# A written instruction order replaced by another: late DMAs and dearer tiling turns in the plan, 96 DMA semaphores

## The chip, the core and the metric

The kernel runs on one core of one Trainium2 chip. The core has five engines with a queue of their own: TensorE (PE in the profile; its weight loads are shown as PEld), VectorE (DVE), ScalarE (ACT), GpSimd (POOL) and SyncE (SP), which issues nearly all DMAs here. The metric is the device time of one execution in microseconds.

## The reference

Four sublayers run one after the other over 2048 tokens of width 448, in bf16: attention, GLU, attention, GLU, with the same weights for both attentions and for both GLUs.

```python
def _A_ref(x, mem0, Wq, Wk, Wv, Wo, seg_len):      # 64 segments of 32 tokens, 16 heads of 256
    mem = mem0                                     # 8 memory rows
    for s in range(n_seg):
        xs = x[:, s * seg_len:(s + 1) * seg_len, :].copy()
        h = jnp.concatenate([mem, xs], axis=1)     # 40 rows
        q, k, v = ...                              # h times Wq, Wk, Wv
        scores = jnp.einsum('bhqe,bhke->bhqk', q, k) * scale
        scores = jnp.where(mask[None, None], scores, -1000000000.0)
        p = _softmax(scores, axis=-1)
        o = jnp.einsum('bhqk,bhke->bhqe', p, v)
        o = jnp.einsum('bhte,hed->btd', o, Wo)
        mem = o[:, :M, :].copy()
        outs.append(o[:, M:, :])
...
def _B_ref(x, W_gate, W_up, W_down):
    gate = ...; up = ...
    h = relu(gate) * up
    return jnp.einsum('bsf,fd->bsd', h, W_down)

x = x + _A_ref(_layernorm(x, axis=-1), ...)
x = x + _B_ref(_layernorm(x, axis=-1), ...)
x = x + _A_ref(_layernorm(x, axis=-1), ...)
x = x + _B_ref(_layernorm(x, axis=-1), ...)
```

The memory rows of a segment need those of the segment before, so the memory's part is a chain of 63 links in each attention layer. The other 32 rows of a segment hang on the chain but not on each other.

## The kernel before

**What is computed where.** The weights are folded first: `weights` loads Wq and Wk, turns them on TensorE (`transposes`, profile lines L1084 and L1085) and multiplies them per head into `A` (`product`, L1102), and Wv with Wo into `Bsb`. After that each head needs `h A h^T` for its scores and `p h B` for its output.

`chain(step)` runs one link of the memory chain for both attention layers together, the second layer `LAG` = 7 segments behind the first. In series: `mT` times `A` into PSUM (L1270), four evictions into `Usb`, small transposes by a selection matrix (`middle`, L1427) with evictions, scores (L1450), a softmax on VectorE and ScalarE, a transpose of the probabilities, the product with the rows (L1514 and L1518), and the product with `Bsb` (L1307), whose four column groups are added to `Osum` and written to `Ohi`. From there the new memory goes back to `mT`, and by small DMAs into the row tiles `HR`. Most steps also carry rows of the second layer that ride along (`Tr`, `Pr`, `PTr`); `PTr` is made by a transposing DMA.

`tiles(step, t)` does the work of a tile of 128 tokens every fourth step: four `att_group` calls (L1603 into `Ug`, scores L1632, softmax in `Tx` and `Px`, a transposing DMA `Tx<-Px`, products L1514 and L1518, output L1670), then `norm` into a `G` tile (two transposing DMAs `G<-xn`) and the GLU (`glu_units` L1692, `glu_down` L1710).

**The tiling of TensorE.** Its matmuls use five shapes of tile (rows x columns): 64x128 for L1603 and L1692, 64x32 for L1270, 128x32 for L1307, 128x64 for some products of weights, and the full 128x128 for the rest. A matmul of another shape than the one before it is called a turn here.

**What sets the order.** `_Sched.add` records every operation with the engines that could run it and what it needs. `schedule` then follows four tables that stand in the source, written by a search outside the kernel:

- `ORDER`: 9235 entries, one per operation. An entry v means operation v // 5 on engine v % 5 (0 TensorE, 1 ScalarE, 2 VectorE, 3 GpSimd, 4 SyncE). It fixes the order on each engine, and which engine evicts a PSUM bank.
- `BANKS`: the PSUM bank of each allocation, in the same order (8 banks).
- `FILLS`: at such a place in the order, so many matmuls on a zeroed tile (`warm`, L178) whose result nobody reads.
- `TURN`: at which step the parts of a tile were recorded.

`emit` puts each engine's operations in that order and adds semaphore waits. All engines run in order: one that waits holds what stands behind it. Each DMA in order of recording gets a semaphore slot, n modulo `N_DMA`, and needs the DMA n - `N_DMA` landed before it is issued:

```python
            if n >= self.N_DMA:
                o.deps[self.dmas[n - self.N_DMA]] = True
```

`turn_dma` (L1044) issues the transposing DMAs `G<-xn`, `Tx<-Px` and `PTr<-Pr` on SyncE, `dma` (L1049) the plain ones.

Of the kernel before, what the change touches and what calls it, by code (L numbers as in the profile page):

```python
# [50 lines left out]
class _Sched:  # L51
# [5 lines left out]
    N_DMA = 48  # L57
# [13 lines left out]
    def add(self, engs, cost, fn, r=(), w=(), prio=None, dma=0, alloc=(), room=(), mode=0, now=None, part=(0, 0), after=()):  # L71
# [46 lines left out]
        if dma:  # L118
            n = len(self.dmas)
            o.slot = n  # L120
            if n >= self.N_DMA:
                o.deps[self.dmas[n - self.N_DMA]] = True
# [157 lines left out]
def bass_interleave_layers__memory_aug_recurrent_mem_tr__glu_gated_reglu__prompt_kernel(  # L280
# [477 lines left out]
FILLS = {1969: (12, 2, 0), 9083: (15, 0, 0), 9211: (7, 0, 0), 9217: (10, 0, 0)}  # L758
# [1079 lines left out]
```

## Time and profile before

| | before |
|---|---|
| median of 3 runs | 1563.47 us (1560.84 to 1564.4) |
| time of the profiled execution | 1558.09 us |
| its span, first to last instruction | 1556.3 us |
| granted TensorE clock in it | 0.998 |
| TensorE busy (matmul) | 1508.1 us |
| VectorE, ScalarE, GpSimd busy | 1127.3, 820.6, 58.0 us |
| moved by DMA | 49.84 MB |

A matmul's end is modelled in the trace, and matmuls overlap: a 64x128 one is shown with 216 ns, but the next starts about 28 ns later. So TensorE's busy time contains short waits, and its cost is read from starts. A wait for several semaphores is put down to what came last by the profile. Where the engine named had long been done, it was another, often a DMA.

### The profile page before, as it was taken

How to read it: one execution, taken by the hardware profiler on the slowest of the kernel's cores; microseconds unless marked ns; L12 is line 12 of the kernel's file. 1: busy time of each engine (PE TensorE's matmuls, PEld its weight loads, DVE VectorE, ACT ScalarE, POOL GpSimd, SP SyncE). 2: the span in 40 equal slices, each digit the busy share in tenths (PEclk: the TensorE clock that was granted, in tenths of full speed). 3: DMA queues.
4: the chain of work that ended last, by engine and by line, in shares of the span. 5: the costliest groups of instructions: out<-in, count | busy, mean ns of one | idle time of the engine just before them, and what ended most of it. 6: DMA issues, size and time to landing. Idle time of an engine off the chain costs nothing.

```text
span 1556.3 us, 84947 instructions
## 1 busy us (share of the span) xinstructions
PE 1508.1 (97%) x38530; PEld 1097.1 (70%) x38530; DVE 1127.3 (72%) x3284; ACT 820.6 (53%) x2297; POOL 58.0 (4%) x241
## 2 busy tenths in 40 slices
PE   8999999999999999999999999999999999999998
PEld 6676766667667677767767676777768676777766
DVE  8755678677876777778776778677776777767764
ACT  6754556455555545445555555555555556544442
POOL 1000000000000000000000000000000000000000
PEclk9999999999999999999999999999999999999999
DMA  9422000100100100101001101001001111010101
GB/s 266 145 81 56 12 22 16 18 17 17 23 16 19 27 18 20 19 21 24 19 20 21 29 13 28 17 20 25 20 18 19 26 17 28 19 18 21 20 18 27
DMA packets 114167, 49.84 MB, mean 32 GB/s; under 512 B 82824, under 2 KB 113808, under 8 KB 113808
## 3 DMA queue, kind: packets, MB, share of 16 engines
q1 hardware_dynamic: 113168, 44.15, 12.5%
q8 instruction: 304, 4.98, 1.3%
q14 instruction: 55, 0.45, 0.1%
q10 hardware_dynamic: 640, 0.26, 0.1%
HBM read 21.35 MB, written 1.84 MB: 15 GB/s over the span
## 4 chain that ended last, share of the span: by engine, by line
PE 85%; DVE 7%; DMA 5%; ACT 1%; issue 1%; SPq 1%; ACTq 0%; DVEq 0%; POOL 0%
PE psG L1670 14%; PE psG L1603 14%; PE psG L1692 11%; PE psC L1307 11%; PE psC L1270 7%; PE psG L1710 5%; PE psG L1270 3%; PE psG L1514 3%; PE psG L1102 2%; PE psG L1632 2%; PE psC L1427 2%; DMA Tx<-Px 2%; PE psC L1450 1%; PE psC L1514 1%; PE psG L1427 1%
## 5 line engine op out<-in xcount | busy, mean ns | idle before, releaser
L1670 PE MATMUL psG<-Bsb,YT 128*128 128x448 bf16 x1288 | 277.3, 353 | 0.0
L273 ACT ACTIVATE Ug<-psG 64x128 bf16<-64x128 f32 (+2 forms) x441 | 156.7, 370 | 88.9 <-PE psG L1603 72.2
L1692 PE MATMUL psG<-G,glu 64*128 64x128 bf16 x5838 | 184.6, 216 | 11.5 <-DMA G<-xn 5.0
L1307 PE MATMUL psC<-Bsb,YTm 128*32 128x448 bf16 (+2 forms) x4144 | 187.6, 333 | 0.9 <-issue 0.5
L1692 PEld LDWEIGHTS psG<-G,glu 64*128 64x128 bf16 x5838 | 172.6, 94 | 22.0 <-issue 7.9
L1603 PE MATMUL psG<-HT,A 64*128 64x128 bf16 x3332 | 175.7, 217 | 0.3 <-ACT Bsb L273 0.3
L1670 PEld LDWEIGHTS psG<-Bsb,YT 128*128 128x128 bf16 x1288 | 111.1, 97 | 91.2 <-issue 9.5
L1270 PE MATMUL psG<-A,mT 64*32 64x448 bf16 x4424 | 173.7, 350 | 0.3 <-issue 0.3
L1270 PE MATMUL psC<-A,mT 64*32 64x448 bf16 x3416 | 152.8, 350 | 1.9 <-DVE Tr L1476 1.0
L1603 PE MATMUL psG<-HX,A 64*128 64x128 bf16 x2499 | 150.1, 217 | 0.0
L1307 PEld LDWEIGHTS psC<-Bsb,YTm 128*32 128x32 bf16 x4144 | 102.5, 97 | 65.2 <-DVE YTm L276 2.3
L276 DVE CAST Ug<-psG 64x128 bf16<-64x128 f32 (+2 forms) x265 | 111.1, 429 | 23.1 <-PE psG L1603 18.9
L1697 ACT ACTIVATE hG<-psG 128x512 bf16<-128x512 f32 (+1 forms) x125 | 67.9, 543 | 105.3 <-PE psG L1692 99.1
L1603 PEld LDWEIGHTS psG<-HT,A 64*128 64x128 bf16 x3332 | 116.9, 95 | 8.9 <-issue 5.3
L1324 DVE TENSOR_TENSOR Osum<-psC,Osum 32x448 f32<-32x448 f32 (+2 forms) x120 | 73.2, 610 | 68.7 <-ACT Osum L1322 65.9
L276 DVE CAST YT<-psG 128x448 bf16<-128x448 f32 x148 | 90.2, 618 | 41.3 <-PE psG L1518 40.2
L273 ACT ACTIVATE YT<-psG 128x448 bf16<-128x448 f32 x214 | 107.7, 540 | 20.5 <-PE psG L1518 18.2
L1270 PEld LDWEIGHTS psC<-A,mT 64*32 64x32 bf16 x3416 | 76.5, 92 | 53.8 <-ACT mT L273 3.0
L1270 PEld LDWEIGHTS psG<-A,mT 64*32 64x32 bf16 x4424 | 90.3, 92 | 22.0 <-ACT mT L273 1.9
L1710 PE MATMUL psG<-glu,hG 128*128 128x448 bf16 x434 | 97.5, 353 | 0.2 <-DVE hG L1698 0.2
L1698 DVE TENSOR_TENSOR hG<-hG,psG 128x512 bf16<-128x512 bf16 (+1 forms) x113 | 68.9, 617 | 39.3 <-ACT hG L1697 38.4
L1603 PE MATMUL psG<-l,A 64*128 64x128 bf16 x2919 | 97.2, 216 | 0.0
(294 smaller groups left out, 2910.8 us busy)
## 6 DMA issues: line engine op xcount, KB each, us to landing
Bsb<-in_A_Wq_dram SPq DMA_DIRECT2D x6, 384.0 KB
Bsb<-in_A_Wk_dram SPq DMA_DIRECT2D x6, 384.0 KB
glu<-in_A_Wv_dram SPq DMA_DIRECT2D x6, 384.0 KB
Tsb<-Ohi SPq DMA_DIRECT2D x128, 7.0 KB
X<-in_A_x_dram SPq DMA_DIRECT2D x16, 112.0 KB
glu<-in_A_Wo_dram SPq DMA_DIRECT2D x4, 448.0 KB
out_dram<-X SPq DMA_DIRECT2D x16, 112.0 KB
glu<-in_B_W_gate_dram SPq DMA_DIRECT2D x14, 112.0 KB
```

Of the source, the lines that this page charges most:

```text
L273: return E.activation(out, i, ACT.Copy, scale=1.0 if scale is None else scale)
L276: return E.tensor_copy(out, i)
L1270: i = E.matmul(ub[v].ap()[32 * j:32 * j + 32, 0:D], lhsT=self.mT[rw, b, :], rhs=self.A[rw, b, a0:a0 + D], start=(b == 0), stop=(b == 6), t ...
L1307: x = E.matmul(bo.ap()[32 * j:32 * j + 32, 0:d1 - d0], lhsT=self.YTm[:, q, :], rhs=self.Bsb[:, chunks[q], d0:d1], start=(i == 0), stop=(i ...
L1324: s.add("dve", dv_cost(n), lambda E, e, j=j, a_=a_, part=part: E.tensor_tensor(a_, part(j), a_, ALU.add), r=[bo], w=w, part=(j, 0), **P)
L1514: return E.matmul(ps[:, n * q:n * q + n], lhsT=HR[rows, KM + 128 * q:KM + 128 * q + 128], rhs=PT, start=True, stop=True, tile_position=(b, 0))
L1603: i = E.matmul(ub[v].ap()[:, 128 * n:128 * n + 128], lhsT=self.A[rw, b, a0:a0 + 128], rhs=HT[rw, b, :, 0:SEG] if b < 4 else HX[rw, b - 4, ...
L1670: i = E.matmul(bo.ap()[:, 0:D], lhsT=YT[:, c, :], rhs=self.Bsb[:, 14 * g + c, :], start=(g == 0 and c == 0), stop=(g == 3 and c == 13))
L1692: i_ = E.matmul(two[v].ap()[:, 128 * c:128 * c + 128], lhsT=self.Wgu[rw, b, f0:f0 + 128], rhs=G[rw, b, :], start=(b == 0), stop=(b == 6), ...
L1697: s.add("act", 169 + 0.84 * N, lambda E, e, dst=dst, z=two[0], N=N: E.activation(dst, z.ap()[:, 0:N], ACT.Relu), r=[two[0]], w=[("hG", i, ...
L1698: s.add("dve", dv_cost(N), lambda E, e, z=two[1], N=N, dst=dst: E.tensor_tensor(dst, dst, z.ap()[:, 0:N], ALU.mult), r=[two[1]], w=[("hG", ...
L1710: i_ = E.matmul(bk.ap()[:, 0:D], lhsT=hG[:, c, :], rhs=self.Wd[:, c, :], start=(c == 0), stop=(c == NFC - 1))
```

## The change

No operation is added, taken away or resized. Three of the tables and one number are replaced:

- `N_DMA`, the number of DMA semaphores, goes from 48 to 96.
- `ORDER` is written anew by the search, which planned each small DMA to land later than before and counted more for a turn of the tiling. It holds the same 9235 operations. An operation stands 23 places from where it stood before on average (half of them 13 or fewer). 553 operations move from VectorE to ScalarE and 509 the other way, 28 from VectorE to GpSimd and 21 the other way.
- `BANKS` follows the new order (2667 allocations).
- `FILLS` has 2 places instead of 4, 19 matmuls instead of 44.

In the built programs, TensorE's stream has 588 turns after and 574 before. Its first five groups of transposes are those of operations 55, 58, 61, 64 and 81 before, and of 64, 61, 58, 81 and 55 after. (In `ORDER`, 275 is operation 55 on TensorE, 320 is 64.)

```diff
@@ _Sched
-    N_DMA = 48
+    N_DMA = 96
@@ ORDER
-    158, 37, 163, 92, 266, 259, 42, 102, 168, 47, 112, 271, 639, 173, 52, 178, 122, 275, 62, 183, 264, 95, 67, 188,
-    282, 290, 193, 539, 2448, 105, 287, 297, 2453, 544, 305, 302, 72, 312, 549, 320, 317, 327, 554, 405, 332, 559, 77, 345,
...
+    158, 37, 163, 92, 266, 259, 42, 102, 168, 47, 112, 271, 639, 173, 52, 178, 122, 62, 183, 264, 67, 188, 77, 193,
+    72, 539, 82, 2448, 87, 2453, 544, 549, 320, 554, 305, 326, 290, 559, 312, 331, 297, 564, 405, 316, 275, 302, 411, 569,
...
@@ BANKS
-    2, 0, 3, 4, 2, 3, 4, 2, 5, 6, 3, 2, 4, 5, 3, 2, 4, 5, 3, 2, 4, 5, 3, 0, 2, 4, 3, 5, 2, 6, 4, 3, 7, 5, 6, 2, 4, 3, 5, 2,
...
+    2, 3, 4, 5, 2, 3, 0, 4, 1, 2, 5, 3, 4, 6, 2, 3, 4, 5, 2, 3, 4, 5, 2, 3, 4, 2, 3, 5, 6, 7, 3, 4, 2, 5, 6, 0, 2, 4, 3, 5,
...
@@
-FILLS = {1969: (12, 2, 0), 9083: (15, 0, 0), 9211: (7, 0, 0), 9217: (10, 0, 0)}
+FILLS = {1389: (7, 1, 0), 1965: (12, 2, 0)}
```

896 rows, old and new, of tables (BANKS, ORDER) are left out of this document.

## The prediction

> **What bounds the kernel now.** I read the page first: how full each engine is, then its chain.
>
> ```profile
> span 1556.3 us, 84947 instructions
> ...
> PE 1508.1 (97%) x38530; PEld 1097.1 (70%) x38530; DVE 1127.3 (72%) x3284; ACT 820.6 (53%) x2297; POOL 58.0 (4%) x241
> ...
> PE 85%; DVE 7%; DMA 5%; ACT 1%; issue 1%; SPq 1%; ACTq 0%; DVEq 0%; POOL 0%
> ```
>
> TensorE (PE) bounds it everywhere. The change keeps every operation, so what it can move is the time in which PE streams nothing: 1556.3 - 1508.1 = 48.2 us of idle, plus costs that hide inside "busy". The next view groups PE's instructions by line and shape; behind the last bar stands PE's idle time just before the group, and what ended it.
>
> ```profile
> L1692 PE MATMUL psG<-G,glu 64*128 64x128 bf16 x5838 | 184.6, 216 | 11.5 <-DMA G<-xn 5.0 <-ACT Osum L1322 2.4 <-DVE str L1480 1.8
> L1514 PE MATMUL psG<-Tx,HR 40*128 40x128 bf16 x726 | 39.3, 218 | 10.7 <-DMA Tx<-Px 7.5 <-DVE Usb L276 1.3 <-ACT Osum L1322 0.8
> L1514 PE MATMUL psG<-Tx,l 40*128 40x128 bf16 x360 | 19.7, 216 | 3.3 <-DMA Tx<-Px 1.8 <-DVE Ug L276 1.4
> L1514 PE MATMUL psG<-PTr,l 40*128 40x128 bf16 x189 | 14.6, 219 | 1.3 <-DMA PTr<-Pr 1.3
> L1514 PE MATMUL psC<-PTr,l 40*128 40x128 bf16 x183 | 14.2, 217 | 2.5 <-DMA PTr<-Pr 1.7 <-DVE stm L1466 0.3 <-issue 0.2
> L1427 PE MATMUL psG<-Selm,Usb 128*128 128x64 bf16 x424 | 24.4, 193 | 1.0 <-DVE Usb L276 0.8
> ```
>
> The first five groups read a tile that a transposing DMA made: G (the normed tile, for the GLU), Tx (softmax of a tile) and PTr (softmax of a riding step). Before them PE idles 11.5 + 14.0 + 3.8 = 29.3 us, six tenths of all its idle time. Some of it is put down to DVE or ACT. The timeline of one such wait shows why I count that too:
>
> ```profile
> 285.84 2.56 SPq L1044 DMA_TRANSPOSE G<-xn  x2
> ...
> 290.61 0.23 DVE L1480 TENSOR_REDUCE str<-Tr 128x2 f32<-128x80 f32 x1 [0.34 <-ACT Tr L1479]
> ...
> 290.95 1.24 PE L1692 MATMUL psG<-G,glu 64*128 64x128 bf16 x38 [1.79 <-DVE str L1480]
> ```
>
> `glu_units` reads G, the weights and two PSUM banks, never `str`. The reduction merely ended at that moment; what came late was G's second transpose, 290.95 - 285.84 = 5.1 us after the first was issued. So 5.1 us from the pair's issue to its use is the price that an order must cover with other matmuls.
>
> **The change part by part.** *Room for the transposes.* In both written orders I took, for each transposed tile, the matmuls that stand between the last one that feeds it and the first one that reads it, at the intervals of the rows below (L1692 196 in 5.58 us, or 0.028 us each; L1710 ten in 1.90, or 0.190 each), and subtracted the VectorE work that stands between the first and last VectorE operation of that tile's softmax or norm, at the durations of the trace. What is left is the room for queue and landing; the wait above has 4.2 us of it.
>
> G: 12 of 32 readers have under 6 us before, and 9 of those wait; after, 4 of 32 do, and none has under 5 (six before). Tx: 8 of 96 have under 3.5 us before, 2 after; but between 3.5 and 5 there are 16 before and 23 after. PTr: 7 of 62 under 3.5 before, 3 after. With the mean wait of each class of room in the trace before, put on the counts after, G goes from 11.5 to 3.2 us, Tx from 14.0 to 11.6, PTr from 3.8 to 2.3: **12.2 us less**. Bounds: nothing, if the landings were as late as the new plan fears, and 29.3 if all of it goes.
>
> *What is late next.* Where such a wait goes, PE arrives sooner at whatever follows, and the evictions and softmax chains of the same stretch do not get faster. Of the 48.2 us idle, 5.1 belong to the start (4.75 and 0.39, rows below) and 29.3 to the transposes; the other 13.8 are for VectorE, ScalarE and GpSimd, a third of what is not the start. I let a third of the gain come back in such waits: **+4.1 us**, between 0 and all 12.2.
>
> *Evictions near their readers.* In the written order, 23 of the 396 instruction groups on L1427 (the transposes of the step's `Usb`) stand closer to `Usb`'s evictions than these take, against 14 before. The row above has 1.0 us of idle there; by the count it would be 1.6. The longest of those waits is 0.5 us:
>
> ```profile
> PE psG L1427 <- DVE Usb L276: 0.8, 2, 0.5
> ...
> SPq L1049 <- DMA out_dram<-X: 12.3, 7, 2.6
> ```
>
> 23 times 0.5 would be 11.5, so between +0.6 and +10.5; I take **+2.0**, near the row.
>
> *Turns of the tiling and dummies.* PE's stream changes its tile shape 574 times before and 588 times after: the search did not lower the count. The end of the timeline has the price:
>
> ```profile
> 1532.26 5.47 PE L1670 MATMUL psG<-Bsb,YT 128*128 128x448 bf16 x28
> 1537.66 3.30 PE L1692 MATMUL psG<-G,glu 64*128 64x128 bf16 x112
> ...
> 1542.38 2.07 PE L1710 MATMUL psG<-glu,hG 128*128 128x448 bf16 x10 [0.16 <-DVE hG L1698]
> 1544.28 0.72 PE L178 MATMUL psC<-warm 128*128 128x128 bf16 x10
> 1544.93 5.64 PE L1692 MATMUL psG<-G,glu 64*128 64x128 bf16 x196
> 1550.51 2.82 PE L1710 MATMUL psG<-glu,hG 128*128 128x448 bf16 x14
> ```
>
> 28 matmuls at 0.190 are 5.32 us, but the next shape starts after 5.40: a turn takes about 0.09. Ten dummies (0.056 each) and a turn, 0.65, say the same. 14 more turns: **+1.3 us**. The Trainium skill (TensorEngine Tiling (Array Packing), Key Properties) says that changing the tiling mode drains TensorE, and its page TensorE: Matmul & The Clock Gate (Single matmul latency) has about 166 ns of fixed latency on a matmul that stands alone; if a turn laid all of that bare, 14 would cost, as an estimate from that page, 2.3 us. The rows show about half of it per turn, and the sum uses the rows.
>
> The dummies of `FILLS` go from 44 matmuls to 19. The two fills shown stand where PE waits for the last G; in the order after, 8.3 us of real matmuls stand there, and PE needs 1544.93 - 1537.66 = 7.27 us of cover: **-1.4 us** (25 at 0.056), 0 if the wait stays without them.
>
> *The start.* The first transposes on PE are of other weights than before.
>
> ```profile
> 0.74 1.00 SPq L1049 DMA_DIRECT2D Bsb<-in_A_Wq_dram  x2
> ...
> 1.78 1.02 SPq L1049 DMA_DIRECT2D Bsb<-in_A_Wk_dram  x2
> 1.98 1.27 ACTq L1069 DMA_DIRECT2D Bsb<-in_A_Wk_dram  x2
> ...
> 4.75 0.80 PE L1084 MATMUL psG<-ident,Bsb 128*128 128x128 bf16 x6 [4.75 <-DMA Bsb<-in_A_Wq_dram]
> ...
> 8.36 0.80 PE L1084 MATMUL psG<-ident,Bsb 128*128 128x128 bf16 x6 [0.39 <-DMA Bsb<-in_A_Wq_dram]
> ...
> 9.19 1.37 PE L1102 MATMUL psG<-glu 128*64 128x448 bf16 x12
> ```
>
> Before, PE begins with the first load of Wq, 4.0 us after its issue. After, it begins with the second load of Wk (issued about 2.3) and its tails (about 2.6), so at 6.3 to 6.6, 1.6 to 1.9 later. From 4.75 to 9.19 PE does five groups of seven, 3.75 us of work at the first rows' 0.107 each, so about 0.7 of that stretch is waiting that a later beginning does not repeat: **+1.0 us**, between 0 and 1.9.
>
> *The rest.* 96 DMA semaphores let DMA n be issued before DMA n-48 has landed. SyncE's own waits name one DMA landing, the store of X (12.3 us in 7, row above), and that is the reuse of X's buffer, which stays; PE waits for nothing behind it. I cost it at nothing, with no more than the 2.6 us of its longest wait on either side. 553 evictions move from VectorE to ScalarE and 509 back, 28 to GpSimd and 21 back: VectorE loses 51 of 3284. PE covers that, and it helps the chains that trigger the transposes; no extra credit.
>
> Sum: -12.2 + 4.1 + 2.0 + 1.3 - 1.4 + 1.0 = **-5.2 us**. The profiled execution took 1558.1 us with its span of 1556.3, and would come to 1552.9. It stands 5.4 below the runs' median of 1563.5, so I put the difference on the median: **1558.3 us**.
>
> **The rivals.** *Given back in full.* Each wait that goes is replaced by one as long: -12.2 + 12.2 + 2.9 for the other terms, 1566.4. For it: VectorE is 72% full, and Tx has 25 of 96 readers under 5 us (24 before). Against: G has rooms of 6 us and more for 28 readers, 20 before. It is also the case in which the late plan does not reach the chip.
>
> *Slower: the recurrent step.* 70 steps each run `Usb` through two evictions, L1427, scores and softmax in series. If the new order lets other evictions stand ahead of `Usb`'s, each step grows; at 0.25 us (half the longest wait in the row) that is 17.5 us, -12.2 + 0.9 (start, turns and dummies) + 17.5 = +6.2, **1569.7**. It decides over no change from (12.2 - 0.9) / 70 = 0.16 us per step. Against: only 23 of 396 groups are that near, where it needs every step.
>
> *All the transposes' waits go*, 29.3 us, with a third back: -19.5 + 2.9, **1546.9**. Against: the Tx counts.
>
> **How the numbers follow.** The forecast has 0.48 (own range 1551 to 1563), given back 0.18, slower 0.22, all gone 0.12. 0.2% is 3.1 us, about the 3.6 us by which the three runs before differ. Of the forecast, 0.06 lies within that, so faster 0.54, same 0.24, slower 0.22. The range 1546 to 1571 reaches from the best rival to just past the slower one, and takes in the Usb bound only in part.
>
> **What the profile after would show.** PE's idle before L1692 at 3 to 5 us instead of 11.5, before the Tx groups 10 to 13, before PTr 2 to 3; the first matmul at 6.3 to 6.6; PE busy as before within 3 us, and total idle down by about as much as the span. L1427's idle near 2 to 3 us: if it is over 10, the slower rival holds. If G's idle stays near 11, the rooms were no measure of the waits, and the sum is wrong at its first term.

## The result, and the profile after

| | before | after |
|---|---|---|
| median | 1563.41 us (1560.84 to 1564.4, 4 runs) | 1541.03 us (1539.56 to 1542.56, 4 runs) |
| time of the profiled execution | 1558.09 us | 1540.21 us |
| its span | 1556.3 us | 1538.4 us |
| PE busy | 1508.1 us | 1508.3 us |
| PE idle (span less busy) | 48.2 us | 30.1 us |

The changed kernel takes 0.9859 of the time, with a 95% interval of 0.9842 to 0.9877: 22.4 us less, where 5.2 were forecast. The direction was right; the size was not, and 1541.0 lies below the range.

PE streams for the same time in these two profiles, so in them all of the gain is idle time that went. The page of the changed kernel shows it in the two lines that answer those of before, busy engines and the shares of the chain that ended last:

```profile
span 1538.4 us, 84907 instructions
...
PE 1508.3 (98%) x38505; PEld 1095.8 (71%) x38505; DVE 1117.7 (73%) x3233; ACT 826.9 (54%) x2341; POOL 59.7 (4%) x248
...
PE 91%; DVE 5%; DMA 1%; ACT 1%; SPq 1%; issue 1%; POOL 0%; POOLq 0%
```

In the chain, DMA falls from 5% to 1%. Where it went is seen in PE's groups by line and shape (behind the last bar: the idle before the group, and what ended it):

```profile
L1692 PE MATMUL psG<-G,glu 64*128 64x128 bf16 x5978 | 190.0, 216 | 1.7 <-DVE Ug L276 0.8 <-DMA G<-xn 0.7 <-ACT Tx L1642 0.2
L1514 PE MATMUL psG<-Tx,HR 40*128 40x128 bf16 x714 | 39.9, 218 | 3.2 <-DMA Tx<-Px 2.1 <-DVE Usb L276 0.8
L1427 PE MATMUL psC<-Selm,Usb 128*128 128x64 bf16 x544 | 31.3, 193 | 1.1 <-DVE Usb L276 0.9 <-ACT lnst L1537 0.2
L1427 PE MATMUL psG<-Selm,Usb 128*128 128x64 bf16 x436 | 24.2, 193 | 1.0 <-DVE Usb L276 1.0
L1514 PE MATMUL psG<-Tx,l 40*128 40x128 bf16 x345 | 19.8, 216 | 0.0
L1427 PE MATMUL psG<-Selr,Usb 128*128 128x64 bf16 x304 | 17.6, 193 | 0.5 <-DVE Usb L276 0.5
L1514 PE MATMUL psG<-PTr,l 40*128 40x128 bf16 x192 | 12.9, 219 | 0.6 <-DMA PTr<-Pr 0.4
L1514 PE MATMUL psC<-PTr,l 40*128 40x128 bf16 x180 | 12.2, 216 | 0.0
L1514 PE MATMUL psC<-Tx,HR 40*128 40x128 bf16 x54 | 6.0, 217 | 0.4 <-issue 0.2 <-ACT YT L273 0.2
L1514 PE MATMUL psC<-Tx,l 40*128 40x128 bf16 x39 | 3.5, 217 | 0.8 <-DMA Tx<-Px 0.7 <-ACT YTm L273 0.2
```

A reader is a group of matmuls that reads a transposed tile; where 190 are counted below, it is the first one of each tile. Idle before the readers goes from 29.3 to 6.7 us: G from 11.5 to 1.7, Tx from 14.0 to 4.4, PTr from 3.8 to 0.6. That is 22.6 less, and little comes back: the start has 6.9 us where it had 5.1, and all groups but the readers and the start together have 12.4 where they had 10.9; L1427, which waits for `Usb`, has 2.6 of these, 1.0 before. The rest of PE's idle time lies behind its last matmul: 4.4 us, 3.0 before. The timeline of PE has the start:

```profile
6.86 0.80 PE L1084 MATMUL psG<-ident,Bsb 128*128 128x128 bf16 x6 [6.86 <-DVE Sel L1006]
7.45 0.31 PE L1085 MATMUL psG<-ident,Bsb 128*128 128x128 bf16 x1
```

How one wait went is seen in the two timelines. Before, a Tx tile was ready when L1645 ended (593.37 + 0.32 = 593.69), but SyncE was still at the plain DMAs that stand ahead of its transpose in the written order. The transpose was issued at 595.68, and PE stood idle for 1.77 us until it could read the tile at 598.98, 3.30 us after the issue:

```profile
590.07 1.99 SPq L1049 DMA_DIRECT2D l<-Ohi  x2
592.11 1.80 SPq L1049 DMA_DIRECT2D HR<-xn  x3
...
593.37 0.32 DVE L1645 TENSOR_TENSOR Px<-Tx,stx 128x160 bf16<-128x160 f32 x1
...
593.95 1.67 SPq L1049 DMA_DIRECT2D Tsb<-Ohi  x2
595.68 3.13 SPq L1044 DMA_TRANSPOSE Tx<-Px  x2
...
598.98 0.34 PE L1514 MATMUL psG<-Tx,l 40*128 40x128 bf16 x6 [1.77 <-DMA Tx<-Px]
```

The wait cost more than its 1.77 us. In the 3.41 us after it the granted TensorE clock (PEclk, behind the busy times) was half of what it was before:

```profile
core 0: us, PE busy (x) PEld busy (x) DVE busy (x) ACT busy (x) POOL busy (x), PEclk, DMA share, GB/s
596.38:599.79 3.41, 1.64 (x42) 1.30 (x42) 1.43 (x5) 0.65 (x2) 0.00 (x0) 1.00 0.21 42
599.79:603.20 3.41, 3.41 (x74) 3.41 (x70) 1.48 (x3) 1.21 (x3) 0.00 (x0) 0.51 0.33 72
```

In the changed kernel the transpose of the same tile is issued as soon as the tile is ready, and PE comes to it 23.14 us later:

```profile
557.38 0.30 DVE L1645 TENSOR_TENSOR Px<-Tx,stx 128x160 bf16<-128x160 f32 x1
...
557.71 1.17 SPq L1044 DMA_TRANSPOSE Tx<-Px  x1
...
580.85 0.34 PE L1514 MATMUL psG<-Tx,l 40*128 40x128 bf16 x6
```

### The profile page after: what moved, and what is told of

The parts are those of the page before. It is cut to its first block, busy times and chain, and to the rows that moved or that the text cites. A ratio compares the mean times of both kernels' runs of the same rounds, so it can differ in the third digit from the quotient of the medians.

```text
span 1538.4 us, 84907 instructions
## 1 busy us (share of the span) xinstructions
PE 1508.3 (98%) x38505; PEld 1095.8 (71%) x38505; DVE 1117.7 (73%) x3233; ACT 826.9 (54%) x2341; POOL 59.7 (4%) x248
## 4 chain that ended last, share of the span: by engine, by line
PE 91%; DVE 5%; DMA 1%; ACT 1%; SPq 1%; issue 1%; POOL 0%; POOLq 0%
PE psG L1670 15%; PE psG L1603 15%; PE psG L1692 11%; PE psC L1307 11%; PE psC L1270 8%; PE psG L1710 6%; PE psG L1270 4%; PE psG L1514 3%; PE psG L1102 3%; PE psG L1632 2%; PE psC L1427 2%; PE psG L1307 1%; PE psG L1427 1%; PE psC L1450 1%; PE psG L1084 1%; PE psC L1514 1%
## 5 line engine op out<-in xcount | busy, mean ns | idle before, releaser
L273 ACT ACTIVATE Ug<-psG 64x128 bf16<-64x128 f32 (+2 forms) x428 | 152.4, 372 | 80.2 <-PE psG L1603 64.7
L1692 PE MATMUL psG<-G,glu 64*128 64x128 bf16 x5978 | 190.0, 216 | 1.7 <-DVE Ug L276 0.8
L1692 PEld LDWEIGHTS psG<-G,glu 64*128 64x128 bf16 x5978 | 176.4, 94 | 14.1 <-issue 9.8
L1307 PE MATMUL psC<-Bsb,YTm 128*32 128x448 bf16 (+2 forms) x3864 | 178.0, 336 | 0.7 <-issue 0.5
L1603 PE MATMUL psG<-HT,A 64*128 64x128 bf16 x3244 | 168.6, 216 | 0.6 <-issue 0.5
L1270 PE MATMUL psG<-A,mT 64*32 64x448 bf16 x4284 | 164.7, 350 | 0.6
L1603 PE MATMUL psG<-HX,A 64*128 64x128 bf16 x2433 | 144.0, 216 | 0.1
L1307 PEld LDWEIGHTS psC<-Bsb,YTm 128*32 128x32 bf16 x3864 | 96.0, 97 | 64.4 <-DVE YTm L276 2.9
L276 DVE CAST Ug<-psG 64x128 bf16<-64x128 f32 (+2 forms) x267 | 110.4, 422 | 18.3 <-PE psG L1603 13.8
L1603 PEld LDWEIGHTS psG<-HT,A 64*128 64x128 bf16 x3244 | 112.1, 94 | 8.0 <-issue 5.5
L276 DVE CAST YT<-psG 128x448 bf16<-128x448 f32 x140 | 85.1, 618 | 39.6 <-PE psG L1518 38.6
L1270 PEld LDWEIGHTS psG<-A,mT 64*32 64x32 bf16 x4284 | 85.3, 92 | 22.9 <-ACT mT L273 1.9
```

The source lines that it names most:

```text
L273: return E.activation(out, i, ACT.Copy, scale=1.0 if scale is None else scale)
L276: return E.tensor_copy(out, i)
L1270: i = E.matmul(ub[v].ap()[32 * j:32 * j + 32, 0:D], lhsT=self.mT[rw, b, :], rhs=self.A[rw, b, a0:a0 + D], start=(b == 0), stop=(b == 6), t ...
L1307: x = E.matmul(bo.ap()[32 * j:32 * j + 32, 0:d1 - d0], lhsT=self.YTm[:, q, :], rhs=self.Bsb[:, chunks[q], d0:d1], start=(i == 0), stop=(i ...
L1603: i = E.matmul(ub[v].ap()[:, 128 * n:128 * n + 128], lhsT=self.A[rw, b, a0:a0 + 128], rhs=HT[rw, b, :, 0:SEG] if b < 4 else HX[rw, b - 4, ...
L1692: i_ = E.matmul(two[v].ap()[:, 128 * c:128 * c + 128], lhsT=self.Wgu[rw, b, f0:f0 + 128], rhs=G[rw, b, :], start=(b == 0), stop=(b == 6), ...
```

## The experiments

Comparisons are with runs of the kernel before on the same chip, whose median lay between 1556 and 1564 us. The theories at the beginning: ROOM (more PE work between a tile's last feeding matmul and its reader), QUEUE (transposes stand shorter behind plain DMAs on SyncE), EVICTIONS (the engines that evict were better shared out).

**The semaphores alone.** The old tables with the new number of semaphores.

```diff
-    N_DMA = 48
+    N_DMA = 96
```

> The order before, with 96 DMA semaphores instead of 48 and nothing else. Three theories for the 22 us that the new order saves. ROOM: more matmul time, less VectorE work, between the operations that feed a transposing DMA and the first matmul that reads it. QUEUE: transposes stood behind other DMAs in SyncE's queue (in the trace before, the mean time from ready to issue is 1.27 us for Tx; after, 0.73), part of it through waits for the DMA 48 earlier. EVICTIONS: 51 operations fewer on VectorE. ROOM and EVICTIONS: 1563.4, within 2 us. QUEUE, if the semaphores do it: 5 us or more faster than before.

1556.14 us, ratio 1.0 (0.9976 to 1.0023). The semaphores carry nothing of the gain. They do have a price: PE's idle time behind the last matmul is 4.4 us here instead of 3.0. It is 4.4 to 4.8 in every profile with 96 of them, the changed kernel's too, and 2.9 to 3.4 in every one with 48 (`emit` ends with a wait for each DMA among the last `N_DMA` operations of SyncE). This is also a second profile of the old order: idle before G, Tx and PTr of 7.5, 12.6 and 6.1 us (26.2 in all, against 29.3), so single classes of waits vary from run to run more than their sum.

**Transposes ahead in SyncE's queue.** Each transposing DMA of the old order is moved right behind the last operation that it needs; 38 of 222 pass 85 plain DMAs. The cut shows the edit in outline.

```diff
 ORDER (old tables, N_DMA = 96)
-    ..., plain DMAs, transposing DMA, ...
+    ..., transposing DMA, plain DMAs, ...
```

> The order before with 96 semaphores, and each transposing DMA moved forward in the written order to the place right behind the last operation that it needs; 38 of 222 so pass 85 plain DMAs on SyncE. All other engines keep their order. ROOM: within 3 us of 1563.4. QUEUE: 8 to 15 us faster, 1548 to 1555, with the idle time before L1692 and L1514 down by as much.

1567.58 us, ratio 1.0092 (1.0061 to 1.0123): slower, which neither theory had. The queue did get shorter for Tx (from ready to issue 0.74 us on average, 1.27 before and 0.73 in the changed kernel), yet Tx's idle only fell to 11.9 us:

```profile
L1514 PE MATMUL psG<-Tx,HR 40*128 40x128 bf16 x726 | 39.7, 220 | 9.7 <-DMA Tx<-Px 4.6 <-DVE YT L276 1.9 <-DVE Usb L276 1.3
L1514 PE MATMUL psG<-Tx,l 40*128 40x128 bf16 x360 | 19.9, 218 | 2.2 <-DVE Ug L276 1.5 <-issue 0.7
```

The groups beyond the transposes' readers and the start have 18.9 us of idle instead of 10.9, and PE's busy time is 1516.2 us instead of 1508.1: six stretches at half the clock lie in this profile, two in that of before. That the plain DMAs which were passed are now late is likely, but was not shown wait by wait. QUEUE by itself is not it.

**The engines of the evictions.** The old order, every operation on the engine that the new order gives it (in outline).

```diff
 ORDER (old places, N_DMA = 48)
-    v = 5 * operation + old engine
+    v = 5 * operation + new engine
```

> The order before, but each operation that can run on two engines runs on the engine that the new order gives it (553 from VectorE to ScalarE, 509 the other way, 28 to GpSimd and 21 back), at its old place. ROOM: no gain; 1563 to 1573, since the places were written for other engines. EVICTIONS: 6 us or more faster.

1603.54 us, ratio 1.0325 (1.0293 to 1.0358). EVICTIONS falls: the choice of engines belongs to its order, and in the old one it costs 47 us, far more than the 0 to 10 that ROOM allowed.

**Transposes that need no tile.** The transposing DMAs read a constant tile, the folded weights, so that they wait for no softmax or norm (the cut shows the edit for Tx).

```diff
-P.rearrange("p g k -> p (g k)"), 65536, r=[("Px", si)],
+self.A[:, 0, 0:256], 65536, r=self.A_all,
```

> The order before, but the transposing DMAs read a piece of the folded weights A instead of the softmax and the normed tile, so they wait for no earlier engine (the attention probabilities and the GLU's input are left out of the result). This measures what the waits for transposes are worth before: 29.3 us of idle by the rows. If a third comes back in the next waits, as the prediction took it: 1563.4 - 19.5 = 1544. If nothing comes back: 1534. If all comes back: 1563.

1549.11 us, ratio 0.996 (0.9939 to 0.9981). G's idle fell to 3.9 and PTr's to 2.6, Tx's stayed at 13.9. The edit freed Tx only in part: its transpose is written into the very tile on which the softmax works, so it still followed the softmax. A weak test; the next one cuts on the readers' side.

**Readers that wait for no transpose.** In both orders all DMAs run as they were, but PE's readers of G, Tx and PTr read a constant tile. First the changed kernel again as a base:

> The changed kernel as it is, beside the kernel before on the chip of these runs, as the base for the next three. Both theories: 0.983 to 0.990 of the kernel before. What is looked at besides is the spread of its runs: an order that leaves room for late landings should vary by less than 5 us where the kernel before varied by 15 us on the chip of the first four experiments. If both vary alike, the chip and not the order made that spread.

1544.6 us (1542.01 to 1546.64), ratio 0.9876 (0.985 to 0.9901). Then the two kernels whose readers wait for no transpose, called blind:

```diff
-rhs=G[rw, b, :],
+rhs=self.A[rw, b, 0:128],
...
-PT[r0:r0 + L, 128 * p:128 * p + 128], 128)
+self.A[r0:r0 + L, 0, 128 * p:128 * p + 128], 128)
...
-r=[k_("Tx")] + hk
+r=self.A_all + hk
```

> Kernel before with every transposing DMA issued as it was, but PE's readers (L1692, and L1514 for Tx and PTr) read a constant tile of the folded weights in place of G, Tx and PTr, so that no matmul waits for a transpose or for the softmax or norm ahead of it. It leaves out the use of the normed tile and of the tiles' probabilities. Theory ROOM (the waits for transposes are the whole difference between the two orders): all of the 26 to 29 us of idle in these groups goes and at most a quarter comes back elsewhere, so 20 to 29 us less than before, 0.981 to 0.987, and level with the changed kernel made blind in the same way within 4 us. Rival REST (the old order also waits more for other things, hidden behind these waits): only 8 to 16 us less, and over 8 us slower than the changed kernel made blind.

> The changed kernel made blind in the same way (readers of G, Tx and PTr read a constant tile; the use of the normed tile and of the tiles' probabilities is left out). ROOM: its 6.7 us of idle in these groups goes, at most a quarter comes back: 5 to 7 us less than the changed kernel, and within 4 us of the kernel before made blind. REST: likewise 5 to 7 us less than the changed kernel, but over 8 us faster than the kernel before made blind.

Kernel before, blind: 1530.53 us, ratio 0.9791 (0.9766 to 0.9816). Changed kernel, blind: 1534.62 us, 0.9814 (0.9793 to 0.9835). So the waits for transposes are worth 1563.97 - 1530.53 = 33.4 us in the old order and 1544.6 - 1534.62 = 10.0 in the new one, both more than expected (20 to 29, and 5 to 7). One part of the surplus is in PE's busy time, which fell with the waits: 1502.2 us in the old order, blind, with no stretch at half the clock, where the profile before had 1508.1 and two. The difference, 23.4, is more than the 19.4 us by which the two orders differ here; without these waits the new order is no faster (4.1 us slower, an uncertainty of about 5). Beyond that uncertainty nothing of the gain is elsewhere. The groups of the old order, blind, show the readers without their waits:

```profile
span 1527.0 us, 84996 instructions
...
L1692 PE MATMUL psG<-A,glu 64*128 64x128 bf16 x5838 | 184.2, 216 | 0.3 <-issue 0.3
L1514 PE MATMUL psG<-A,HR 40*128 40x128 bf16 x726 | 38.9, 217 | 0.1
L1514 PE MATMUL psG<-A,l 40*128 40x128 bf16 x549 | 33.7, 217 | 0.1
```

**The start.** The first five groups of transposes of the weights, with their evictions, back in the old order.

```diff
 ORDER (new)
-    320, ..., 305, ..., 290, ..., 405, ..., 275
+    275, ..., 290, ..., 305, ..., 320, ..., 405
```

> The changed kernel, with the first five groups of transposes of the weights put back into the order of the kernel before (operations 55, 58, 61, 64, 81), so that PE begins with the first load of Wq. If the start costs what the traces show (idle of 6.9 us at the start after, 5.1 before), 1 to 2 us less than the changed kernel, and the first matmul near 4.8 us. Rival: the later begin is caught up by the loads that follow, and the time is the same within 0.5 us.

1540.63 us (1538.77 to 1546.97), ratio 0.9858 (0.9829 to 0.9886), beside 0.9876 of the changed kernel: 4 us less by the medians, with intervals that overlap, so the run can't decide between 1 to 2 us and nothing. The idle at the start is 5.7 us instead of 7.7 (first line; the second is the changed kernel, blind, on the same chip):

```profile
L1084 PE MATMUL psG<-ident,Bsb 128*128 128x128 bf16 x192 | 15.5, 239 | 5.7 <-DMA Bsb<-in_A_Wq_dram 5.7
```

```profile
L1084 PE MATMUL psG<-ident,Bsb 128*128 128x128 bf16 x192 | 15.3, 238 | 7.7 <-DMA Bsb<-in_A_Wk_dram 7.7
```

**Every transpose later.** Two plain DMAs that nobody needs ahead of each of the 222 transposing DMAs (the helper's lines push the later line numbers up by 9, so L1514 reads L1523).

```diff
+            for _ in range(2):
+                ...
+                E.dma_start(self.junk[q:q + 1, c:c + 8], self.ident[q:q + 1, 0:8]).then_inc(self.s.xs, 16)
             return E.dma_start(dst, src, transpose=True)
```

> Kernel before with two plain DMAs of 16 bytes, which nobody needs, issued on SyncE right ahead of each of its 222 transposing DMAs, so that each transpose is issued some 1.2 us later (2 x 0.6 us of issue). Theory ROOM (what differs between the orders is how much PE work stands between a transposed tile's last feeding matmul and its first reader): tiles whose readers had less than 1.2 us to spare now wait. From issue-to-use times less 5.0 us for a G pair and 4.0 for a single one, the added waits sum to at most 109 us; since waits in a row overlap, 40 to 90 us more than the kernel before. Rival QUEUE (what differs is that SyncE is busy with plain DMAs when a tile gets ready): the added 266 us on SyncE's queue hit both orders alike, both lose the same within 10 us.

> The changed kernel with the same two plain DMAs ahead of each transposing DMA. ROOM: by the same count at most 84 us, 25 to 65 us more than the changed kernel, and at least 12 us less loss than the kernel before has. QUEUE: the same loss as in the kernel before within 10 us.

1722.61 us (ratio 1.1047, 1.0956 to 1.1138) and 1690.34 us (1.0775, 1.0706 to 1.0843): about 160 and 146 us lost, far more than both theories had. The transposes came 2 to 3 us later after their input was ready, not 1.2. And not all of the loss is idle time: in the two profiles some 90 us each passed at half the clock, and PE's busy time rose to 1547.2 and 1548.2 us. At that dose 78 of 190 readers wait in the old order and 60 in the new one, and the comparison tells little. Half the dose followed, with the changed kernel as a base on the same chip:

> Kernel before with one plain DMA of 16 bytes, which nobody needs, ahead of each of the 222 transposing DMAs on SyncE (half the dose of the earlier pair). With two, the transposes were issued 2.3 to 3.2 us later after their input was ready, not 1.2, since the additions queued behind each other, and both orders lost nearly alike (160 and 146 us). Theory MARGIN (the new order has more to spare for its tightest readers, some 1 to 2 us, and no more): at half the dose the delay stays within that margin, so the kernel before loses 30 to 60 us, and at least 12 us more than the changed kernel. Rival ALIKE (the new order's gain is of another kind than spare time): both lose the same within 8 us, about half of what the double dose cost, 70 to 80.

> The changed kernel with the same one plain DMA ahead of each transposing DMA. MARGIN: 15 to 35 us more than the changed kernel, at least 12 less of a loss than the kernel before has. ALIKE: 70 to 80 us more, the same loss within 8 us.

> The changed kernel as it is, as the base of these runs on their chip: 0.985 to 0.989 of the kernel before.

1614.34 us (ratio 1.0357, 1.0312 to 1.0401), 1588.75 us (1.0185, 1.0139 to 1.0232), and 1539.0 us for the changed kernel (0.9875, 0.9841 to 0.991). The old order lost 55.0 us, the new one 49.8. The difference, 5 us with an uncertainty of about 11, is nearer to ALIKE but does not exclude MARGIN's 12, and ALIKE's 70 to 80 us was too much for both. Part of the loss is the clock again: 30.7 and 27.3 us at half of it, none in the profile of the changed kernel here. One group of each, old order first, then the new one:

```profile
L1523 PE MATMUL psG<-Tx,HR 40*128 40x128 bf16 x726 | 39.6, 219 | 23.2 <-DMA Tx<-Px 15.8 <-DVE Usb L278 1.6 <-issue 1.4
```

```profile
L1523 PE MATMUL psG<-Tx,HR 40*128 40x128 bf16 x714 | 40.3, 218 | 14.0 <-DMA Tx<-Px 11.9 <-ACT Osum L1331 1.3 <-ACT hG L1706 0.7
```

With the half dose the new order already waits more (43.3 us of idle before all readers of transposed tiles, 40 of them waiting) than the old one without any (29.3, 33 waiting): its advantage is worth less than one such DMA ahead of each transpose. Why the old order did not lose more than the new one is open.

**The price of a turn.** In the changed kernel 100 single dummy matmuls between full-tile groups, once of another tile shape (128x32, 200 turns more), once of the same (none). They are entries of `FILLS`, whose last number chooses the shape: 1 in the first run, as shown, and 0 in the second. (In the built programs L1514 and L1518 have the shape 64x128 too, not the full one; the counts of turns include that.)

```diff
-FILLS = {1389: (7, 1, 0), 1965: (12, 2, 0)}
+FILLS = {1389: (7, 1, 0), 1965: (12, 2, 0), 611: (1, 7, 1), 761: (1, 7, 1), 873: (1, 7, 1), ...}
```

> The changed kernel with 100 single dummy matmuls, each of another tile shape than its neighbours, put between full-tile groups of PE: 200 more turns of the tiling. At 0.093 us a turn by the starts in the traces and about 0.056 us a matmul: 18.6 + 5.6 = 24 us more than the changed kernel, less what falls into its idle time, so 17 to 25, and 14 to 20 more than the next run. Rival: a turn lays bare the 166 ns that the Trainium skill gives for a lone matmul (TensorE: Matmul & The Clock Gate, Single matmul latency): 200 of them 33 us, as an estimate from that page.

> The changed kernel with the same 100 single dummy matmuls at the same places, but of the full tile shape like their neighbours: no more turns. 100 at 0.056 us: 3 to 6 us more than the changed kernel. The difference between this run and the one before it, divided by 200, is the price of a turn: 0.07 to 0.10 us if the rows are right, about 0.17 if all of the lone matmul's latency is laid bare.

1568.25 us (ratio 1.0026, 1.0004 to 1.0047) and 1553.01 us (0.9921, 0.9894 to 0.9948). The difference, 15.2 us by 200, is 0.076 us a turn, with an uncertainty of about 0.027; PE's busy time in the two profiles (1534.6 and 1514.1 us, of which one stretch at half the clock makes 1.7) gives 0.094. The rows' 0.09 lie within the uncertainty. The estimate from the Trainium skill (TensorE: Matmul & The Clock Gate, Single matmul latency), 166 ns laid bare at each turn, does not: it would be 33 us. The 100 dummies of the full shape missed their forecast of 3 to 6 us: 1553.01 us is 8.4 more than the changed kernel had on this chip, with an uncertainty of about 6. Its profile says the same, with 1514.1 us of busy time where the changed kernel had 1505.4 to 1508.3, so a single one between other groups seems to cost more than the 0.056 that it has in a row of ten.

**Start and dummies together.** The new order with the old start (`ORDER` as in the run with the old start) and without its 19 dummies.

```diff
-FILLS = {1389: (7, 1, 0), 1965: (12, 2, 0)}
+FILLS = {}
```

> The changed kernel with the first five groups of transposes in the order of the kernel before and without its 19 dummies. Theory by the rows: 1.8 to 2.0 us of idle less at the start (5.9 against 7.7 us in the blind pair), and 19 x 0.056 = 1.1 us of dummies less where PE doesn't wait there: 2 to 3 us less than the changed kernel, the fastest version. Rival: the later start and the dummies lie over loads of weights that PE waits for anyway, so the time is that of the changed kernel within 1 us.

1542.1 us (ratio 0.9897, 0.9864 to 0.9929), beside 1539.0 of the changed kernel: not faster. The idle at the start did fall, from 8.0 to 6.0 us, but G has 5.5 us where the changed kernel had 2.2 on this chip, and Tx 4.7 where it had 2.5:

```profile
L1692 PE MATMUL psG<-G,glu 64*128 64x128 bf16 x5978 | 190.1, 216 | 5.5 <-DMA G<-xn 4.7 <-issue 0.8
```

Whether the earlier start causes these waits or one run differs from another is not settled. No version that does all of the work beats the changed kernel beyond the uncertainty.

**A shorter softmax.** Five steps of the Tx softmax work on 32 columns instead of 160, in both orders; the other columns are left out. One of the five:

```diff
-E.tensor_tensor(P[:, :, 0:L], T[:, :, :], bc(rc), ALU.mult)
+E.tensor_tensor(P[:, :, 0:8], T[:, :, 0:8], rc.unsqueeze(2).to_broadcast([128, 4, 8]), ALU.mult)
```

> Kernel before with the softmax of every Tx tile cut from 160 to 32 columns in five of its steps (the two reductions, the subtraction, the exponential, the last product; the other columns are left out). Four VectorE steps of 0.31 to 0.32 us and one ScalarE step of 0.34 us each get about 0.13 us shorter (a 128x32 copy on VectorE took 0.19), so each Tx tile is ready some 0.65 us sooner, with the queue and the matmuls as they were. Theory NEED (the prediction held the time from a tile's last feeding matmul to its transpose's issue fixed, and the new order shortened it for Tx from 5.7 to 4.8 us on average, with the tightest readers gaining about half a microsecond): cutting it here brings Tx's idle from 12.6 to 14.0 down to 4 to 7 us, and 6 to 12 us less than the kernel before. Rival LANDING (the spread of landing times, 2.4 to 4.9 us from issue to use, sets these waits): Tx's idle stays over 9 and the gain is under 4 us.

> The changed kernel with the same cut of the Tx softmax from 160 to 32 columns. NEED: its 2.5 to 5.8 us of idle before Tx readers goes to under 2, 1 to 5 us less than the changed kernel (0.985 to 0.9875 of the kernel before in three comparisons), and the gap to the kernel before with the same cut shrinks from about 20 to 12 to 17 us. LANDING: the gap stays at 18 to 23 us.

1558.04 us (ratio 0.9984, 0.9966 to 1.0002) and 1540.01 us (0.9855, 0.9831 to 0.9878). Old order: 2 to 3 us less, which the interval doesn't tell from nothing, with Tx's idle at 10.5 us; in the new order Tx's idle is 3.2 us. The gap between the orders is 18.0 us. That is what LANDING had, and NEED's 6 to 12 us are excluded. But the steps did get shorter by 0.11 to 0.13 us each, and the tile ready sooner by only 0.27 us on average (4.16 instead of 4.43 from the last feeding matmul), since the operations of other tiles stand between the steps:

```profile
L1641 DVE TENSOR_TENSOR Tx<-Tx,stx 128x32 f32<-128x32 f32 x96 | 17.5, 187 | 1.4
L1645 DVE TENSOR_TENSOR Px<-Tx,stx 128x32 bf16<-128x32 f32 x96 | 17.4, 185 | 1.1
```

## Why the prediction was wrong in size

**What held.** The gain is the waits for G, Tx and PTr: without them, in the blind pair, none is left, to within about 5 us. PE's busy time was the same in the two profiles (1508.1 and 1508.3), though other profiles of the two orders have 1503.7 to 1506.2. The semaphores, put at nothing, cost 1.4 us at the end and nothing else that shows. The wait put down to `str` was for G: blind, L1692 has 0.3 us of idle. The slower rival (the recurrent step) did not come: L1427 has 2.6 us, the forecast 2 to 3. That its size was met is luck, since the old order has 3.8 us there in its second profile, where it had 1.0 in the first. "Given back in full" is refuted too.

**The step that failed: the first term, 12.2 us less waiting, and in it Tx.** The blind pair has 23.4, and the rows of the two traces 22.6. By class:

| | idle before | forecast | idle after | in two more profiles of the changed kernel |
|---|---|---|---|---|
| G | 11.5 | 3.2 | 1.7 | 3.9, 2.2 |
| Tx | 14.0 | 11.6 | 4.4 | 5.8, 2.5 |
| PTr | 3.8 | 2.3 | 0.6 | 1.5, 0.5 |

G came out near its forecast, PTr somewhat below it. Tx was missed by 7 us. The prediction measured a room in the written order, gave each class of room the mean wait it had in the trace before, and put these means on the new counts. But a room held two things at once, the delay until SyncE issues the transpose and the landing, and the mean of a class contained the old order's delays. With the rooms unchanged, tiles of the new order waited less: of Tx readers with 3.5 to 5 us of room, 6 of 16 waited for 4.1 us before, and 4 of 23 for 3.7 after; under 3.5 us, 5 of 8 for 6.0 before, and 0 of 2 after. From ready to issue Tx took 1.27 us on average before and 0.73 after (over 2 us in 19 of 96 tiles, then 9), and from the last feeding matmul to ready 4.43 and 4.11.

The measure that does separate the orders is what is left for the landing alone: from the issue of a transpose to the moment at which its reader would have begun without its wait. It can be read from the trace, but the written order does not show it.

| | readers with under 3.5 us left, of 190 | sum of what they lack | measured idle before the readers |
|---|---|---|---|
| before | 44 | 31.7 us | 29.3 us |
| before, 96 semaphores | 42 | 28.3 us | 26.2 us |
| after | 14 | 7.9 us | 6.7 us |
| after, second comparison | 13 | 7.0 us | 11.2 us |
| after, third comparison | 16 | 6.7 us | 5.2 us |

A single landing time of 3.5 us tells the orders apart, and gives the waits of these profiles to within 4.2 us. The 3.5 was chosen to fit, near the middle of what waiting readers show (2.4 to 5.1 us from issue to use, 3.30 in the timeline above). What makes 44 into 14 is not one queue: SyncE's part alone took 2 us from Tx (with 8 lost elsewhere), and the softmax's 0.27 us took 2 to 4. What is left has three parts at each tile: the time from the last feeding matmul to the moment at which the reader could begin, less the chain up to ready, less the delay up to the issue. Taken tile by tile from the two traces, no part of the new order helps alone: put into the old order, the new time up to the reader makes the sum of what is lacking 60.4 us, the new chain 44.8 and the new delays 53.4, where the old order has 31.7; all three together make the 7.9 of the table. So the gain is in how well the three fit each other at the same tile. This is a count on traces; no run isolated a part, and moving readers alone in the old order was not tried on the chip.

**The second term, a third given back: +4.1.** By it 23 us would have brought back 8. Idle in all other groups but the start rose from 10.9 to 12.4 us, 1.5, and L1427 alone makes that. (The 13.8 us from which the third was taken also held the 3.0 behind the last matmul, where no wait can come back.) In the blind run of the old order 29 us of waits went and the same groups have 15.7 us, 5 more. A fifteenth to a sixth, not a third.

**The smaller terms**, +2.0 (`Usb`), +1.3 (turns), -1.4 (dummies) and +1.0 (start), +2.9 in all, are what should separate the orders when no reader waits. The blind pair has +4.1, with about 5 of uncertainty: not contradicted, and not confirmed singly. L1427 rose by 1.6. A turn's 0.09 lies within what was measured, 0.076 with an uncertainty of 0.027. PE began at 6.86 us, not at 6.3 to 6.6, and the idle at the start rose by 1.8, not 1.0; in all profiles it is 4.8 to 6.6 us with the old start and 6.9 to 8.0 with the new one.

**The median.** The difference of 5.4 us between the profiled execution and the median was carried over. After, they differ by 0.8 (1540.21 and 1541.03). So the miss of 17.3 us is, by the two traces, 10.4 in the first term, 4.2 in the second (nothing came back outside L1427) and 4.6 here, and about 2 the other way in the start, the end and the rest.

The best rival, all of the transposes' waits gone, was the nearest (1546.9). That is partly luck: it had all 29.3 us go, where 22.6 did, and a third come back, where next to nothing did, and the two errors work against each other.

## What to carry to other kernels

When a written order is replaced, do not carry the mean waits of the old order over to the new one: work out for each reader what is left for the landing after its queue and its chain, and sum what is lacking against a landing time read from the old trace. This needs the new order's times, from a simulation or a trace; the written order alone does not give them. Cutting the dependence on the readers' side, in both versions, prices a class of waits at once (33.4 against 10.0 us here) and shows whether anything else differs. A wait's price is not read from its queue: shortening SyncE's queue alone made the kernel slower, since PE then waited more elsewhere. Nor is it the idle time alone, where the clock falls after a wait.

## What the runs showed of the hardware

- The old order's time varied far more from run to run on some chips than the new one's: 1549.5 to 1564.1 us in 20 runs on one chip; on another 1546.7 to 1565.3 in 11 runs, where the changed kernel had 1537.8 to 1540.0 in 6. On a third it had 1557.8 to 1570.7 in 14 runs and the changed kernel 1542.0 to 1546.6 in 4, and on the chip of the result the old one stayed within 3.6 us in 4 runs. An order with 44 tight readers is exposed to differing landings; that this is the cause was only argued. The granted clock takes a part: among the 11 runs the fastest had 1.0 and the slowest 0.995, which at 1508 us of busy time makes about 7.5 us, an estimate.
- A wait of PE can be followed by a stretch of 3.41 us, or a multiple of it, at half the granted clock. The profile before has two (after waits of 2.17 and 1.77 us), that of the changed kernel two (2.11 and 1.25 us), the blind ones none, the one with transposes ahead in the queue six, and the old order with one added DMA per transpose eight; not every wait of that length has one. Such a stretch costs about half its length: PE's busy time runs from 1502.2 to 1548.2 us over the 17 profiles of the two orders that have neither exchanged engines nor 100 added matmuls, but less half of the time at half the clock it is 1501 to 1507 in all of them.
- From issue to use, a transposing DMA whose reader waited took 2.4 to 5.1 us in the five profiles of the two orders.
- A plain DMA of 16 bytes ahead of each transpose costs 0.65 us on SyncE, yet 222 of them cost 50 to 55 us of kernel time, and 444 of them 146 to 160, where the granted clock also fell to 0.973 or 0.974:

```profile
559.81 0.65 SPq L1051 DMA_DIRECT2D junk<-ident  x1
560.51 1.69 SPq L1052 DMA_TRANSPOSE G<-xn  x1
562.24 0.66 SPq L1051 DMA_DIRECT2D junk<-ident  x1
562.94 1.18 SPq L1052 DMA_TRANSPOSE Tx<-Px  x1
```
